# Attention with hashed masks and a gated MLP on one core: the product with v once per half of the queries

## The chip, the cores and the metric

One core of a Trainium2 chip runs the whole program. The metric is the device time of one execution in microseconds, as the median of several runs. The engines go by short names: PE (TensorE, matmuls), PEld (its weight loads), DVE (VectorE), ACT (ScalarE), POOL (GpSimd) and SP (SyncE, which issues most DMAs). SBUF is the working memory; PSUM, into which PE writes, has eight banks of 128 partitions x 512 numbers of 4 bytes.

## The reference

```python
# attention: q, k, v (4, 8, 768, 64), proj (64, 6)
q_bucket, k_bucket = number made of the 6 bits (x @ proj > 0)
mask   = q_bucket[:, :, :, None] == k_bucket[:, :, None, :]
scores = np.where(mask, q @ k.T / sqrt(64), -1e9)
scores = scores - max over the keys
attn   = exp(scores); attn = attn / (sum over the keys + 1e-9)
x      = attn @ v, heads side by side                  # (4, 768, 512)

# gated MLP
h    = gelu_tanh(x @ w_in)                             # 512 -> 1024
u, v = halves of h
v_n  = (v - mean) / sqrt(var + 1e-6) * g_ln
v_s  = einsum('ts,bsd->btd', w_sg, v_n) + b_sg         # mixes the 768 positions
out  = x + (u * v_s) @ w_out
```

Everything is 32-bit floats. The kernel splits most operands into a high part of reduced precision and a remainder, so that one exact product is two to four cheaper matmuls.

## The kernel before

**Order.** The kernel first collects all its work as groups (`plan.add(engine, cost, prio, fn, reads, writes)`) and then lets `Plan.order` write one order for every engine: a list scheduler with a planned duration for each group. At each step it takes the engine and the group that can start earliest, and among the groups that can start then (or a little later, `SOON`) the one with the lowest `prio`, its due time. The planned durations change no instruction, only this order; on the chip each engine then works through its own list in order and waits on semaphores where an operand or a buffer isn't ready. For PE the planner adds `TURN_PE` when a group's `form` differs from that of the group before. There are three forms before the change: `"row"` (64 rows of the array per matmul, two heads side by side), `"col"` (64 columns, two heads side by side) and `None` (everything else).

**Buffers.** `ring(shape, dtype, tag, bufs)` gives tiles that reuse one another in turn: the tile number i waits until all users of number i - bufs are through. `plan.slot` gives a PSUM bank out of a set instead; the planner picks the bank that is free first. Of several groups of an engine that want such a bank and could otherwise start, only the one with the lowest `prio` may be taken.

**Attention.** Two heads make a pair; 16 pairs, each with two halves of 384 queries, so 32 halves. `prepare` loads q and k, transposes and splits them (`parts`, L476 to L483) and computes the hash features (`features`, L498 and L501), which are extra rows that push a score down where the buckets differ. `largest` (L518, L525) computes scores with queries as rows, 384 keys at a time, and reduces the maximum on DVE; `shift` (L533 to L546) writes the maxima of a half back as a feature row. `weigh` (L562 to L583) then handles a chunk: two blocks of 128 keys by 384 queries and two heads. It computes the scores with keys as rows (four matmul pairs for each block), takes the exp on ACT into four tiles `p`, multiplies them with v into the accumulator `av` (L574, `product`), and adds them up over the keys on POOL (`sum`, L583). A half has three chunks, so `product` is called three times per half, each time for two of the six key blocks, all accumulating into `av`. `v` has a column for the mean and `p` a column of ones beside its 384. `finish` (L599 to L622) sums over partitions (`total`, L599), copies `av` out (`un`, L604), inverts the sums by way of small DMAs through DRAM (`s`, `sq`, `r`, `rs`) and writes the half of x to DRAM.

The due times: chunk number g is due at 2g, its product `AVP` = 3.75 later, `finish` `FINP` = 1.7 later, and the maxima run `AHEAD` = 5 chunks ahead. The 16 pieces of w_in (`weight_job`, L339 to L366, mostly on DVE) are spread over the pairs.

PSUM in this stage: one bank for `av` (pool `ps_t`, `NAV` = 1), seven banks that all other tiles share (pool `ps_s`, tags g0 to g6, `ps_tile`). The tiles `p` are a ring of 16.

**MLP.** For each of four batches: `load_x` (L687 to L692), `hidden_v` (L757 to L773: matmuls, gelu, layer norm), `hidden_u` (L789: matmuls and gelu), `gate` (L807 to L818) and `project` (L833 to L843). `hidden_v` of batch 0 comes at the end of the attention (`HID`) and still uses the seven shared banks. Then the attention's pools close, and the MLP has its own PSUM pools: `ps_h` as a ring of four banks, `ps_vs` as a ring of two (both in pool `pm`) and `ps_o` as a ring of two (pool `po`). With batch 0, w_sg is transposed and split (`gate_weights`, L708 to L725) and w_out is split (`out_weights`, `weight_job` again, tiles with names from `ow` on).

Of the kernel before, what the change touches and what calls it, by code (L numbers as in the profile page):

```python
# [25 lines left out]
NAV = 1  # L26
# [7 lines left out]
class Plan:  # L34
# [8 lines left out]
    TURN_PE = 0.09  # L43
# [59 lines left out]
    def order(self):  # L103
# [32 lines left out]
        while len(out) < len(G):  # L136
# [26 lines left out]
            if e == "PE":  # L163

                work = g["c"] + (self.TURN_PE if g["form"] != form else 0.0)
# [58 lines left out]
def kernel(  # L224
# [179 lines left out]
    ps_t, ps_s = Pool("ps_t", "left", PSUM), Pool("ps_s", "left", PSUM)  # L404
    ftp = ps_t.pool.tile([P, 512], F32, tag="av", name="ftp", bufs=NAV)
# [12 lines left out]
    if True:  # L418
        def w_tile(shape, dt, tag):
            return early.ring(shape, dt, tag)  # L420

        ps_slots = {i: 0.0 for i in range(8 - NAV)}

# [13 lines left out]
        NPT = 16  # L437
# [29 lines left out]
        def parts(st, s, prio):  # L467

            hh, lo, raw, fac = st.hi[s], st.lo[s], st.raw[s], (SCALE, 1.0)[s]
            for hf in range(2):  # L470
# [15 lines left out]
                plan.add(PE, 0.38, prio, tr, [raw, (hh, hf), (lo, hf)], [tp])  # L486
# [3 lines left out]
        def features(st, s, prio):  # L490
            hh, lo, ft = st.hi[s], st.lo[s], st.ft[s]
            for hf in range(2):
# [11 lines left out]
                plan.add(PE, 0.58, prio, project, [(hh, hf), (lo, hf), (ft, hf)], [fp])  # L504
                plan.add(DVE, 0.67, prio, sign, [fp], [(ft, hf)])

        def largest(st, t, prio):
# [13 lines left out]
            for kh in range(2):  # L521
                plan.add(PE, 0.36, prio + 0.01 * kh, lambda kh=kh: mm(kh),
                         [(st.hi[0], hf), (st.hi[1], kh), (st.ft[0], hf), (st.ft[1], kh)], sc[kh], form="row")
                for j in range(2):
                    plan.add(DVE, 0.56, prio, lambda j=j, kh=kh: nc.vector.tensor_reduce(  # L525
                        mx()[:, kh, i, j:j + 1], sc[kh][j]()[:, :SH], axis=AX.X, op=ALU.max, negate=True),
                        [sc[kh][j]], [(mx, (kh, j, i))])

        def shift(st, hf, prio):
# [12 lines left out]
            plan.add(PE, 0.35, prio, spread, [m], [tp])  # L542
# [5 lines left out]
        def weigh(st, hf, k0, prio):  # L548

            cs, two = slice(hf * SH, (hf + 1) * SH), (k0, k0 + 1)  # L550
            if k0 == 0:
                st.av = ps_t.ring([P, 512], F32, "av", NAV)
                st.sum = [late.ring([P, SH], F32, "sum", 4) for _ in range(2)]
            av, sums = st.av, st.sum
# [9 lines left out]
            for i, kt in enumerate(two):  # L564
                plan.add(PE, 0.71, prio + 0.01 * i, lambda i=i: mm(i),
                         [(x, hf) for x in (qh, ql, qf)] + [(x, kt // HT) for x in (kh, kl, kf)], sc[i], form="row")
                for j in range(2):
                    plan.add(ACT, 0.53, prio, lambda i=i, j=j: nc.scalar.activation(p[i][j]()[:, :SH], sc[i][j]()[:, :SH], AF.Exp),  # L568
                             [sc[i][j]], [p[i][j]])

            def product():
                for i, kt in enumerate(two):
                    for j in range(2):
                        nc.tensor.matmul(av()[row(j), :SH + 1], st.v()[:, j, kt, :], p[i][j](), start=(kt == 0), stop=(kt == NT - 1))  # L574

            plan.add(PE, 1.48, prio + AVP, product, p[0] + p[1] + [st.v], [av], form="col")
            for i, kt in enumerate(two):
# [3 lines left out]
                for j in range(2):  # L581
                    def add(j=j, i=i, e=e, first=p[0][j] if kt == 1 else sums[j]):
# [3 lines left out]
                             [sums[j]], port=True)  # L586

        def finish(st, hf, prio):
# [12 lines left out]
            plan.add(PE, 0.6, prio, total, sums, [tp])  # L601
# [50 lines left out]
        for n in range(NPAIR):  # L652
            for c in range(NT):
# [5 lines left out]
                if c % HT == HT - 1:  # L659
                    finish(sts[n], hf, 2 * g + FINP)  # L660
# [4 lines left out]
    b3 = pm = po_ = None  # L665
# [16 lines left out]
    def load_x(b, prio):  # L682
        r = []
        for c in range(NC):
# [7 lines left out]
            plan.add(ACT, 0.73, prio + c, lambda x=x, xh=xh: nc.scalar.copy(xh(), x()), [x], [xh])  # L692
            plan.add(M_["xl"], 1.76 if M_["xl"] == POOL else 0.87, prio + c, low, [x, xh], [xl])
# [9 lines left out]
    def gate_weights(prio):  # L703

        sg_v = w_sg.rearrange("(p t) s -> t p s", t=NT)
        for t in range(NT):
            w = tile_of([P, S], F32, "gs", 2 * NF)
            dma(prio + t - 5, 1.09, lambda eng, w=w, t=t: eng.dma_start(w(), sg_v[t]), w=[w], e=ACT)  # L708
            for hf in range(2):
# [17 lines left out]
                plan.add(PE, 0.32, prio + t, tr, [w], [tp])  # L727
# [9 lines left out]
    def gelu2(ps, dst, n, prio, key=None):  # L737

        h2 = tile_of([P, FH], F32, "h2", 2)
        us = n / 960.0  # L740
        plan.add(ACT, us - 0.02, prio, lambda: nc.scalar.activation(h2()[:, :n], ps()[:, :n], AF.Square), [ps], [h2])  # L741
        plan.add(DVE, us + 0.07, prio, lambda: nc.vector.scalar_tensor_tensor(  # L742
            h2()[:, :n], h2()[:, :n], 1.0 / GA, ps()[:, :n], op0=ALU.add, op1=ALU.mult), [h2, ps], [h2])
        plan.add(ACT, us - 0.02, prio, lambda: nc.scalar.activation(h2()[:, :n], h2()[:, :n], AF.Tanh, scale=GC * GA),
# [4 lines left out]
    def hidden_v(xx, prio):  # L749
        zh, zl = tile_of([P, NT, FH], F32R, "zh", 1), tile_of([P, NT, FH], F32R, "zl", 1)  # L750
        for t in range(NT):
            ps, p0 = ps_of("h", 4), prio + t
            ts_ = slice(t * P, (t + 1) * P)
            for c, (xh, xl) in enumerate(xx):
# [4 lines left out]
                plan.add(PE, 0.65, p0 + 0.01 * c, mm, [xh, xl], [ps])  # L759
# [4 lines left out]
            plan.add(DVE, 0.6, p0, lambda y=y, st=st: V.bn_stats(st(), y()), [y], [st])  # L764
# [140 lines left out]
```

## Time and profile before

| | |
|---|---|
| median of 3 runs | 830.72 us (828.22 to 831.31) |
| profiled execution: span from the first to the last instruction | 829.1 us; its own time isn't given beside the span |
| instructions | 15354 |
| busy PE / DVE / POOL / ACT | 795.1 / 602.3 / 449.5 / 415.3 us |
| granted clock of PE, mean | 0.988 of full speed |
| HBM read, written | 47.16 MB, 12.78 MB |
| last product with v (L574) starts | 486.1 us |

PE's busy time is a union of matmul spans, and matmuls are pipelined: a matmul is shown as longer than its share of the engine, and successive ones overlap. What one costs is read from the distance of the starts. A row such as "L574 PE MATMUL av<-p,v 128\*64 128x385" says: line 574, the tile written and those read, the part of the array used (rows\*columns), the shape of the result; one matmul call of 32-bit floats there is recorded as two instructions. The idle time at the end of a row is that of the engine just before the row's instructions, with what ended it.

### The profile page before, as it was taken

To read this page: it belongs to the slowest core of one execution; us is meant where nothing else is said; L and a number is where in the kernel's file an instruction comes from. 1 tells how busy PE (TensorE), PEld (TensorE's weight loads), DVE (VectorE), ACT (ScalarE), POOL (GpSimd) and SP (SyncE) were. 2 spreads that over 40 slices of the span, in tenths; PEclk is the share of its full clock that TensorE was granted. 3 is DMA by queue.
4 is the path that set the end of the run, shared out by engine and by line. 5 is a ranking of instruction groups with operands and counts; after the bars stand their busy time and mean duration, and the time that the engine had idled before them with its cause. 6 is when DMAs were issued, how large, how long until landed. Compare 5 with 4: busy or idle time off the path is not lost.

```text
span 829.1 us, 15354 instructions
## 1 busy us (share of the span) xinstructions
PE 795.1 (96%) x5480; PEld 613.1 (74%) x5480; DVE 602.3 (73%) x1241; ACT 415.3 (50%) x926; POOL 449.5 (54%) x470
## 2 busy tenths in 40 slices
PE   6999999999999999999999997799799999999998
PEld 4766666666666676667667666698689889988996
DVE  6998889998989888998768538888943248516730
ACT  2456566565566656656665655613343135314411
POOL 1478887889868877787887862333105201601130
PEclk9899999999999999999999999799999999999999
DMA  5222441441442233133222011610024220131003
GB/s 152 51 51 74 107 122 34 111 127 36 113 110 57 73 97 91 34 110 78 60 58 60 21 40 41 223 45 25 27 83 134 82 90 1 39 106 47 1 1 127
DMA packets 99308, 60.94 MB, mean 74 GB/s; under 512 B 64288, under 2 KB 91040, under 8 KB 99232
## 3 DMA queue, kind: packets, MB, share of 16 engines
q1 hardware_dynamic: 97920, 56.94, 24.6%
q10 hardware_dynamic: 1312, 3.02, 1.0%
q8 instruction: 43, 0.70, 0.4%
q14 instruction: 33, 0.27, 0.2%
HBM read 47.16 MB, written 12.78 MB: 72 GB/s over the span
## 4 chain that ended last, share of the span: by engine, by line
PE 75%; DVE 19%; DMA 3%; issue 1%; ACT 1%; SPq 1%; DVEq 0%; ACTq 0%
PE g L562 15%; PE av L574 13%; PE ps_vs L807 12%; PE ps_o L833 8%; PE g L518 7%; PE ps_h L789 6%; DVE mx L525 5%; PE ps_h L757 4%; PE g L498 4%; PE g L476 2%; PE g L757 2%; PE g L540 1%; PE g L599 1%; PE ps_o L838 1%; DVE m L534 1%
## 5 line engine op out<-in xcount | busy, mean ns | idle before, releaser
L583 POOL TENSOR_TENSOR sum<-sum,p 128x384 f32<-128x384 f32 x256 | 260.7, 1049 | 61.1 <-ACT p L568 61.0
L525 DVE TENSOR_REDUCE mx<-g 128x1 f32<-128x384 f32 x384 | 187.7, 547 | 51.8 <-PE g L518 51.6
L568 ACT ACTIVATE p<-g 128x384 f32<-128x384 f32 x384 | 160.5, 494 | 104.9 <-PE g L562 97.4
L574 PE MATMUL av<-p,v 128*64 128x385 f32 x768 | 145.4, 500 | 0.0
L574 PEld LDWEIGHTS av<-p,v 128*64 128x64 f32 x768 | 46.6, 136 | 57.2 <-issue 53.6
L562 PE MATMUL g<-hq,hk 64*128 64x384 f32 x384 | 79.8, 389 | 2.4 <-DVE mx L525 2.4
L562 PEld LDWEIGHTS g<-hq,hk 64*128 64x128 f32 x384 | 39.5, 185 | 51.2 <-issue 26.7
L518 PE MATMUL g<-fk,fq 64*128 64x384 f32 x384 | 76.2, 360 | 0.5 <-DVE fk L501 0.2
L742 DVE SCALAR_TENSOR_TENSOR h<-h,ps_h 128x384 f32<-128x384 f32 (+1 forms) x50 | 29.1, 596 | 65.1 <-ACT h L741 64.8
L767 POOL TENSOR_TENSOR mv<-mv,epsr 128x1 f32<-128x1 f32 x24 | 14.8, 619 | 107.6 <-DVE mv L766 107.6
L518 PE MATMUL g<-hk,hq 64*128 64x384 f32 x384 | 71.6, 340 | 0.0
L583 POOL TENSOR_TENSOR sum<-p,p 128x384 f32<-128x384 f32 x64 | 64.3, 1026 | 10.4 <-ACT p L568 10.4
L562 PE MATMUL g<-hq,lk 64*128 64x384 f32 x384 | 68.9, 336 | 0.0
L562 PE MATMUL g<-lq,hk 64*128 64x384 f32 x384 | 68.7, 335 | 0.0
L562 PE MATMUL g<-fq,fk 64*128 64x384 f32 x384 | 68.6, 335 | 0.0
L833 PE MATMUL ps_o<-woh,gs 128*128 128x512 f32 x192 | 65.5, 402 | 0.0
L807 PE MATMUL ps_vs<-wgh,zl 128*128 128x384 f32 x192 | 64.3, 335 | 0.3 <-DVE zl L773 0.3
L807 PE MATMUL ps_vs<-wgh,zh 128*128 128x384 f32 x192 | 64.3, 335 | 0.0
L807 PE MATMUL ps_vs<-wgl,zh 128*128 128x384 f32 x192 | 64.2, 334 | 0.0
L818 POOL TENSOR_TENSOR gs<-gt,gs 128x384 fp32r<-128x384 f32 x32 | 33.3, 1043 | 55.0 <-ACT gs L815 55.0
L690 POOL TENSOR_TENSOR xl<-x,xh 128x768 fp32r<-128x768 f32 x16 | 30.1, 1890 | 47.6 <-ACT xh L692 38.3
L789 PE MATMUL ps_h<-xh,wih 128*128 128x384 f32 x128 | 44.7, 349 | 9.7 <-DVE y L746 8.2
(135 smaller groups left out, 1729.7 us busy)
## 6 DMA issues: line engine op xcount, KB each, us to landing
q<-in_q_dram SPq DMA_DIRECT2D x32, 192.0 KB
k<-in_k_dram SPq DMA_DIRECT2D x32, 192.0 KB
v<-in_v_dram SPq DMA_DIRECT2D x16, 384.0 KB
rs<-r SPq DMA_DIRECT2D x64, 96.0 KB
xs<-xt SPq DMA_DIRECT2D x32, 192.0 KB
x<-xs SPq DMA_DIRECT2D x16, 384.0 KB
rx<-xs SPq DMA_DIRECT2D x96, 64.0 KB
out_dram<-ob SPq DMA_DIRECT2D x24, 256.0 KB
```

What stands on the lines that cost most here:

```text
L498: nc.tensor.matmul(fp()[:, :SH], w[:, s, :], x()[:, cs], start=(i == 0), stop=(i == 2))
L518: nc.tensor.matmul(sc[kh][j]()[:, :SH], x[0]()[row(j), qs], x[1]()[row(j), kh * SH:(kh + 1) * SH], start=(n == 0), stop=(n == 1))
L525: plan.add(DVE, 0.56, prio, lambda j=j, kh=kh: nc.vector.tensor_reduce(mx()[:, kh, i, j:j + 1], sc[kh][j]()[:, :SH], axis=AX.X, op=ALU.max ...
L562: nc.tensor.matmul(sc[i][j]()[:, :SH], x()[row(j), ks], y()[row(j), cs], start=(n == 0), stop=(n == 3))
L568: plan.add(ACT, 0.53, prio, lambda i=i, j=j: nc.scalar.activation(p[i][j]()[:, :SH], sc[i][j]()[:, :SH], AF.Exp), [sc[i][j]], [p[i][j]])
L574: nc.tensor.matmul(av()[row(j), :SH + 1], st.v()[:, j, kt, :], p[i][j](), start=(kt == 0), stop=(kt == NT - 1))
L583: (nc.gpsimd if e == POOL else nc.vector).tensor_add(sums[j](), first()[:, :SH], p[i][j]()[:, :SH])
L757: nc.tensor.matmul(ps(), x()[:, ts_], w[:, c, FH:FF], start=(c == 0 and n == 0), stop=(c == NC - 1 and n == 2))
L789: nc.tensor.matmul(ps()[:, :SH], w[:, c, fs], x()[:, cs], start=(c == 0 and n == 0), stop=(c == NC - 1 and n == 2))
L807: nc.tensor.matmul(vp(), z()[:, t, fs], w()[:, t, cs], start=(t == 0 and n == 0), stop=(t == NT - 1 and n == 2))
L818: nc.gpsimd if e == POOL else nc.vector).tensor_sub(gl()[:, cs], gt(), gh()[:, cs].bitcast(F32)),
L833: nc.tensor.matmul(po(), a()[:, ts_], w()[:, f, :], start=(f == 0 and n == 0), stop=False)
```

## The change

1. The product with v leaves `weigh`. A new function `weighted` is called once per half, behind its third chunk, and multiplies all six key blocks in one group of 12 calls. The 12 `p` tiles of a half are held until then; their ring grows from 16 to 17. The due time is the same 3.75 behind the third chunk.
2. The accumulator `av` is no longer a bank of its own: it is taken from the shared set like any other tile. The set has eight banks, and the MLP uses the same set throughout: the pools `ps_t`, `pm` and `po` and the rings of four, two and two are gone.
3. Planned durations: new figures for most groups, among them a turn cost that depends on the form that is entered, and a form of its own for `total`.

```diff
-NAV = 1
-    TURN_PE = 0.09
+    TURN_PE = {"row": 0.2, "col": 0.14, "col32": 0.14, None: 0.14}
-                work = g["c"] + (self.TURN_PE if g["form"] != form else 0.0)
+                work = g["c"] + (self.TURN_PE[g["form"]] if g["form"] != form else 0.0)
...
-    ps_t, ps_s = Pool("ps_t", "left", PSUM), Pool("ps_s", "left", PSUM)
-    ftp = ps_t.pool.tile([P, 512], F32, tag="av", name="ftp", bufs=NAV)
+    ps_s = Pool("ps_s", "left", PSUM)
+    ftp = ps_s.pool.tile([P, 512], F32, tag="g0", name="ftp", bufs=1)
...
-        ps_slots = {i: 0.0 for i in range(8 - NAV)}
+        ps_slots = {i: 0.0 for i in range(8)}
...
-        NPT = 16
+        NPT = 17
...
             if k0 == 0:
-                st.av = ps_t.ring([P, 512], F32, "av", NAV)
-                st.sum = [late.ring([P, SH], F32, "sum", 4) for _ in range(2)]
-            av, sums = st.av, st.sum
+                st.sum, st.p = [late.ring([P, SH], F32, "sum", 4) for _ in range(2)], []
+            sums = st.sum
...
-            def product():
-                for i, kt in enumerate(two):
-                    for j in range(2):
-                        nc.tensor.matmul(av()[row(j), :SH + 1], st.v()[:, j, kt, :], p[i][j](), start=(kt == 0), stop=(kt == NT - 1))
-
-            plan.add(PE, 1.48, prio + AVP, product, p[0] + p[1] + [st.v], [av], form="col")
+            st.p += p
...
+        def weighted(st, prio):
+
+            st.av, p = ps_tile(), st.p
+            av = st.av
+
+            def product():
+                for kt in range(NT):
+                    for j in range(2):
+                        nc.tensor.matmul(av()[row(j), :SH + 1], st.v()[:, j, kt, :], p[kt][j](), start=(kt == 0), stop=(kt == NT - 1))
+
+            plan.add(PE, 1.3 * HT, prio, product, [t for two in p for t in two] + [st.v], [av], form="col")
...
-            plan.add(PE, 0.6, prio, total, sums, [tp])
+            plan.add(PE, 0.375, prio, total, sums, [tp], form="col32")
...
                 if c % HT == HT - 1:
+                    weighted(sts[n], 2 * g + AVP)
                     finish(sts[n], hf, 2 * g + FINP)
...
-    b3 = pm = po_ = None
+    b3 = None
...
     def ps_of(tag, bufs, shape=(P, FH)):
-        if pm is None:
-            return ps_tile()
-        return (po_ if tag == "o" else pm).ring(list(shape), F32, "ps_" + tag, bufs)
+        return ps_tile()
...
-    end = ps_s.close()
-    pm = Pool("pm", "right", PSUM, end)
-    end = ps_t.close(end)
-    po_ = Pool("po", "right", PSUM, end)
```

Planned durations (us), before and after:

| group | before | after |
|---|---|---|
| transposes of q, k / features, PE | 0.38 / 0.58 | 0.327 / 0.522 |
| scores for the maxima / for the exps, PE | 0.36 / 0.71 | 0.346 / 0.692 |
| maximum, DVE / exp, ACT | 0.56 / 0.53 | 0.55 / 0.495 |
| product, PE | 1.48 three times | 3.9 once |
| spread / total, PE | 0.35 / 0.6 | 0.33 / 0.375 |
| x split: ACT / POOL | 0.73 / 1.76 | 0.83 / 1.88 |
| hidden_v / hidden_u / gate / project, PE | 0.65 / 0.49 / 0.49 / 0.65 | 0.696 / 0.522 / 0.52 / 0.685 |
| w_sg transposes, PE | 0.32 | 0.36 |
| gelu of n columns: ACT, DVE | n/960 - 0.02, n/960 + 0.07 | n/1100 + 0.135 (square) or + 0.155 (tanh), n/960 + 0.15 |
| layer norm: statistics, scale, high part, low part | 0.6, 0.66, 0.6, 0.66 | 0.69, 0.75, 0.72, 0.76 |
| gate: bias, times u (DVE), high (ACT), low (POOL) | 0.47, 0.47, 0.4, 0.96 | 0.56, 0.56, 0.51, 1.03 |
| output copy, ACT | 0.5 | 0.59 |

Due times, `AHEAD`, the engines that each piece runs on and the arithmetic are the same.

More of the change, by code (lines that the diff above doesn't have):

```diff
@@ L521, in largest @@
             for kh in range(2):
-                plan.add(PE, 0.36, prio + 0.01 * kh, lambda kh=kh: mm(kh),
+                plan.add(PE, 0.346, prio + 0.01 * kh, lambda kh=kh: mm(kh),
                          [(st.hi[0], hf), (st.hi[1], kh), (st.ft[0], hf), (st.ft[1], kh)], sc[kh], form="row")
                 for j in range(2):
-                    plan.add(DVE, 0.56, prio, lambda j=j, kh=kh: nc.vector.tensor_reduce(
+                    plan.add(DVE, 0.55, prio, lambda j=j, kh=kh: nc.vector.tensor_reduce(
                         mx()[:, kh, i, j:j + 1], sc[kh][j]()[:, :SH], axis=AX.X, op=ALU.max, negate=True),
@@ L540, in spread @@
                     nc.tensor.matmul(tp()[:, i * P:(i + 1) * P], m()[:, i, :], identr, start=True, stop=True)
-            plan.add(PE, 0.35, prio, spread, [m], [tp])
+            plan.add(PE, 0.33, prio, spread, [m], [tp])
             ft, cs = st.ft[0], slice(hf * SH, (hf + 1) * SH)
@@ L690, in low @@
                 (nc.gpsimd if M_["xl"] == POOL else nc.vector).tensor_sub(xl(), x(), xh().bitcast(F32))
-            plan.add(ACT, 0.73, prio + c, lambda x=x, xh=xh: nc.scalar.copy(xh(), x()), [x], [xh])
-            plan.add(M_["xl"], 1.76 if M_["xl"] == POOL else 0.87, prio + c, low, [x, xh], [xl])
+            plan.add(ACT, 0.83, prio + c, lambda x=x, xh=xh: nc.scalar.copy(xh(), x()), [x], [xh])
+            plan.add(M_["xl"], 1.88 if M_["xl"] == POOL else 0.87, prio + c, low, [x, xh], [xl])
             r.append((xh, xl))
@@ L758, in mm @@
                                          stop=(c == NC - 1 and n == 2))
-                plan.add(PE, 0.65, p0 + 0.01 * c, mm, [xh, xl], [ps])
+                plan.add(PE, 0.696, p0 + 0.01 * c, mm, [xh, xl], [ps])
             y = tile_of([P, FH], F32, "y", 2)
@@ L763, in hidden_v @@
             V = nc.vector
-            plan.add(DVE, 0.6, p0, lambda y=y, st=st: V.bn_stats(st(), y()), [y], [st])
+            plan.add(DVE, 0.69, p0, lambda y=y, st=st: V.bn_stats(st(), y()), [y], [st])
             plan.add(DVE, 0.08, p0, lambda st=st, mv=mv: V.bn_aggr(mv()[:, 0:2], st()), [st], [mv])
@@ L768, in hidden_v @@
                                                                            op=ALU.pow), [mv], [mv])
-            plan.add(DVE, 0.66, p0, lambda y=y, mv=mv: V.scalar_tensor_tensor(
+            plan.add(DVE, 0.75, p0, lambda y=y, mv=mv: V.scalar_tensor_tensor(
                 y(), y(), mv()[:, 0:1], g_bc(), op0=ALU.subtract, op1=ALU.mult), [y, mv, g_bc], [y], port=True)
-            plan.add(ACT, 0.6, p0, lambda y=y, mv=mv, t=t: nc.scalar.mul(zh()[:, t, :], y(), mv()[:, 2:3]),
+            plan.add(ACT, 0.72, p0, lambda y=y, mv=mv, t=t: nc.scalar.mul(zh()[:, t, :], y(), mv()[:, 2:3]),
                      [y, mv], [(zh, t)])
-            plan.add(DVE, 0.66, p0, lambda y=y, mv=mv, t=t: V.scalar_tensor_tensor(
+            plan.add(DVE, 0.76, p0, lambda y=y, mv=mv, t=t: V.scalar_tensor_tensor(
                 zl()[:, t, :], y(), mv()[:, 2:3], zh()[:, t, :].bitcast(F32), op0=ALU.mult, op1=ALU.subtract),
@@ L806, in mm @@
                         for n, (z, w) in enumerate(((zh, wgh), (zh, wgl), (zl, wgh))):
-                            nc.tensor.matmul(vp(), z()[:, t, fs], w()[:, t, cs], start=(t == 0 and n == 0),
+                            nc.tensor.matmul(vp()[:, :SH], z()[:, t, fs], w()[:, t, cs], start=(t == 0 and n == 0),
                                              stop=(t == NT - 1 and n == 2))
-                    plan.add(PE, 0.49, p0 + 0.01 * t, mm, [(zh, t), (zl, t), wgh, wgl], [vp])
-                plan.add(DVE, 0.47, p0, lambda vp=vp, gt=gt, cs=cs: nc.vector.tensor_add(gt(), vp(), b_bc()[:, cs]),
+                    plan.add(PE, 0.52, p0 + 0.01 * t, mm, [(zh, t), (zl, t), wgh, wgl], [vp])
+                plan.add(DVE, 0.56, p0, lambda vp=vp, gt=gt, cs=cs: nc.vector.tensor_add(gt(), vp()[:, :SH], b_bc()[:, cs]),
                          [vp, b_bc], [gt])
                 e = M_["gm"]
-                plan.add(e, 0.96 if e == POOL else 0.47, p0, lambda gt=gt, f=f, cs=cs, e=e: (
+                plan.add(e, 1.03 if e == POOL else 0.56, p0, lambda gt=gt, f=f, cs=cs, e=e: (
                     nc.gpsimd if e == POOL else nc.vector).tensor_mul(gt(), gt(), us[f]()[:, cs]), [gt, (us[f], hf)], [gt], port=True)
-                plan.add(ACT, 0.4, p0, lambda gt=gt, gh=gh, cs=cs: nc.scalar.copy(gh()[:, cs], gt()), [gt], [(gh, hf)])
+                plan.add(ACT, 0.51, p0, lambda gt=gt, gh=gh, cs=cs: nc.scalar.copy(gh()[:, cs], gt()), [gt], [(gh, hf)])
                 e = M_["gl"]
-                plan.add(e, 0.96 if e == POOL else 0.47, p0, lambda gt=gt, gh=gh, gl=gl, cs=cs, e=e: (
+                plan.add(e, 1.03 if e == POOL else 0.56, p0, lambda gt=gt, gh=gh, gl=gl, cs=cs, e=e: (
                     nc.gpsimd if e == POOL else nc.vector).tensor_sub(gl()[:, cs], gt(), gh()[:, cs].bitcast(F32)),
@@ L841, in project @@
             plan.add(PE, 0.43, p0 + 0.1, residual, [rx], [po])
-            plan.add(ACT, 0.5, p0, lambda ob=ob, po=po: nc.scalar.copy(ob(), po()), [po], [ob])
+            plan.add(ACT, 0.59, p0, lambda ob=ob, po=po: nc.scalar.copy(ob(), po()), [po], [ob])
             dma(p0, 0.73, lambda eng, ob=ob, t=t: eng.dma_start(ov[:, t, :], ob()), [ob])
@@ L872 @@
     plan.run(tc)
-    for p in (b3, b2, b1, po_, pm):
+    for p in (b3, b2, b1, ps_s):
         p.pool.release()
```

20 lines of the change are left out of this document (10 added, 10 removed).

## The prediction

> **What bounds the kernel now.** I read the page first: the busy shares, the slices and the chain that ended last.
>
> ```profile
> PE 795.1 (96%) x5480; PEld 613.1 (74%) x5480; DVE 602.3 (73%) x1241; ACT 415.3 (50%) x926; POOL 449.5 (54%) x470
> ...
> PE   6999999999999999999999997799799999999998
> ...
> DVE  6998889998989888998768538888943248516730
> ...
> PE 75%; DVE 19%; DMA 3%; issue 1%; ACT 1%; SPq 1%; DVEq 0%; ACTq 0%
> PE g L562 15%; PE av L574 13%; PE ps_vs L807 12%; PE ps_o L833 8%; PE g L518 7%; PE ps_h L789 6%; DVE mx L525 5%; PE ps_h L757 4%; PE g L498 4%; PE g L476 2%; PE g L757 2%; PE g L540 1%; PE g L599 1%; PE ps_o L838 1%; DVE m L534 1%
> ```
>
> TensorE is busy nearly everywhere and holds 75% of the chain. VectorE holds 19% and is close to full through the attention, which is the first 24 slices. So I cut the span at the stage borders; the columns are busy microseconds (instructions) of PE, weight loads, DVE, ACT and POOL, then the granted clock and the DMA.
>
> ```profile
> 100.00:200.00 100.00, 97.02 (x804) 65.77 (x800) 90.25 (x173) 64.16 (x153) 81.36 (x81) 1.00 0.32 88
> 200.00:300.00 100.00, 98.73 (x812) 67.69 (x813) 89.58 (x171) 61.08 (x148) 76.87 (x79) 1.00 0.35 90
> 300.00:400.00 100.00, 97.96 (x812) 66.12 (x812) 86.82 (x166) 60.88 (x147) 78.16 (x79) 1.00 0.29 75
> 400.00:486.00 86.00, 85.96 (x715) 56.45 (x709) 54.24 (x107) 55.14 (x132) 71.66 (x73) 1.00 0.18 48
> 505.00:605.00 100.00, 85.19 (x429) 77.39 (x429) 87.93 (x216) 42.01 (x87) 29.58 (x39) 0.93 0.23 76
> 605.00:830.00 225.00, 220.43 (x1161) 199.98 (x1159) 96.34 (x183) 73.96 (x135) 47.59 (x45) 1.00 0.21 65
> ```
>
> In the attention (to about 486) TensorE is the bound, with VectorE some ten per cent behind it. From 505 to 605 TensorE is idle for 14.8 us and VectorE is the fuller one. After 605 TensorE is alone again. A saving on TensorE inside the attention therefore counts, until VectorE is full.
>
> **Term 1: fewer products.** First the cost of one product, from the timeline of TensorE and of its weight loads (start, duration, in us):
>
> ```profile
> 212.27 0.34 PE L518 MATMUL g<-fk,fq 64*128 64x384 f32 x2
> 212.44 0.34 PE L518 MATMUL g<-hk,hq 64*128 64x384 f32 x2
> 212.72 1.51 PE L574 MATMUL av<-p,v 128*64 128x385 f32 x8
> 213.09 0.14 PEld L574 LDWEIGHTS av<-p,v 128*64 128x64 f32 x2 [0.18 <-issue]
> 213.41 0.14 PEld L574 LDWEIGHTS av<-p,v 128*64 128x64 f32 x2 [0.18 <-issue]
> 214.16 0.44 PE L562 MATMUL g<-hq,hk 64*128 64x384 f32 x2
> 214.44 0.34 PE L562 MATMUL g<-hq,lk 64*128 64x384 f32 x2
> 214.61 0.35 PE L562 MATMUL g<-lq,hk 64*128 64x384 f32 x2
> ```
>
> Score matmuls (64*128, two side by side in the rows of the array) start 0.17 apart: 212.27, 212.44, and 214.44, 214.61. The four calls of a product appear as 8 matmuls in four pairs, and the weight loads of successive pairs start 0.32 apart; the plan's new figure for four pairs is 1.3, and I take it. From 212.44 to 214.44 are 2.00 us: one score step, the product, one score step. Overhead of the change of form there and back: 2.00 - 2 x 0.17 - 1.30 = 0.36 us. The matmuls themselves stay: 768 before and after.
>
> ```profile
> L574 PE MATMUL av<-p,v 128*64 128x385 f32 x768 | 145.4, 500 | 0.0
> ...
> 204.47 0.82 PE L476 MATMUL g<-ident,k 128*128 128x128 f32 x6
> 205.22 1.51 PE L574 MATMUL av<-p,v 128*64 128x385 f32 x8
> 206.66 0.53 PE L599 MATMUL g<-sum,ones 128*32 128x192 f32 x8
> ```
>
> 768 / 8 = 96 products, three for each of 32 halves. After the change there are 32 with 24 matmuls each, so 64 visits to the other form go. Not each removes two changes between scores and product: the one at 205.22 stands between transposes and the sums, which differ from one another anyway, and there only its own tail, 1.44 - 1.30 = 0.14, is sure to go. Ends: 64 x 0.14 = 9.0 and 64 x 0.36 = 23.0. Most lie between scores as in the first fence, so I take 0.30: **-19.2 us**, all of it in TensorE's own order of work, with nothing else lying beside it.
>
> **Term 2: VectorE in the attention.** What TensorE waits for there now, and what VectorE does in 55 to 400 (columns of the second fence as in the stage table; of the third: count, busy, mean ns, idle before):
>
> ```profile
> PE g L540 <- DVE m L534: 3.5, 6, 1.1
> PE g L562 <- DVE mx L525: 2.4, 5, 0.7
> PE g L476 <- DVE mx L525: 1.5, 1, 1.5
> ```
>
> ```profile
> 55.00:400.00 345.00, 337.62 (x2785) 229.91 (x2785) 303.95 (x581) 212.53 (x509) 270.63 (x272) 1.00 0.33 86
> ```
>
> ```profile
> L525 DVE TENSOR_REDUCE mx<-g 128x1 f32<-128x384 f32 x280 | 137.1, 547 | 33.8 <-PE g L518 33.6
> L620 DVE TENSOR_TENSOR xt<-un,rs 128x384 f32<-128x384 f32 x23 | 16.9, 734 | 0.8 <-DMA rs<-r 0.8
> ```
>
> The waits are 7.4 us. In the stretch of 345 us are 23 halves (one L620 each). Each loses 2 x 0.30 = 0.60, so it shrinks by 13.8 to 331.2, VectorE goes from 88% to 92%, and its idle time from 41.0 to 27.2. If waits grow as that idle time shrinks (41.0 / 27.2 = 1.5), they become 11.1: **+4 us**. Ends: -7.4 (no wait is left; the eighth bank is free for scores except while a product and its copy hold it) and +13.8 (VectorE's idle time can't shrink at all). POOL, 270.63 of 345, would go to 82%. Its additions are no later relative to anyone: what waits for them is the total, once per half, and a tile is reused only 17 exps later.
>
> The product now needs a bank that it must win like any other tile; before it had its own. It holds one for 12 pairs, 3.9 us, and the copy L604 frees it, so seven banks remain for scores meanwhile, as many as now, and eight otherwise. I cost that at nothing, covered by the same seven banks.
>
> The exps: 12 of 17 tiles of a half are held until its product, five are left, and the next chunk takes four. The product's due time (3.75 behind its last chunk's, chunks 2 apart) puts it behind one further chunk and ahead of the second one, so exps need not wait: 0. The one more tile and its memset: 0, at the start beside the DMA wait.
>
> **Term 3: shared banks behind the attention.** TensorE's waits from 486 to 620, and the stretches at half clock:
>
> ```profile
> PE ps_h L789 <- DVE y L746: 8.2, 5, 3.9
> PE ps_h L716 <- DVE wgl L725: 2.8, 3, 2.3
> PE ps_h L716 <- DVE u L746: 1.9, 2, 1.0
> PE ps_h L789 <- DVE u L746: 1.6, 1, 1.6
> ```
>
> ```profile
> 530.00:540.28 10.28, 7.72 (x31) 6.17 (x30) 9.72 (x19) 6.08 (x14) 6.18 (x5) 0.50 0.42 130
> 598.30:601.70 3.40, 3.29 (x10) 3.29 (x11) 3.30 (x10) 1.06 (x4) 0.95 (x2) 0.50 0.01 2
> ```
>
> ```profile
> 506.71 0.44 PE L789 MATMUL ps_h<-xh,wih 128*128 128x384 f32 x1 [1.01 <-DVE y L746]
> ...
> 510.90 0.45 PE L789 MATMUL ps_h<-xh,wih 128*128 128x384 f32 x1 [1.83 <-DVE y L746]
> ...
> 517.00 0.44 PE L789 MATMUL ps_h<-xh,wih 128*128 128x384 f32 x1 [1.58 <-DVE u L746]
> ```
>
> Each of these is a matmul that waits for the reader of a bank in a ring of four (ps_h), while the banks of ps_vs and ps_o stand empty. With one set of eight, TensorE can run four tiles further ahead; the three waits shown, 1.0 + 1.8 + 1.6 = 4.4, come first in the stage and go. The later ones sit behind VectorE, 87.93 of 100 us busy with work that the change does not touch: when banks come free, what is late next is VectorE's gelu and weight splitting. After waits the clock falls to half: of 7.72 and 3.29 busy us at 0.50, half (5.5) is lost. Ends: 0, and -12 (VectorE's idle time in that stretch). I take **-5**.
>
> **Term 4: planned durations.** They change no instruction, only the order that the planner writes. Several come closer to the rows: exp goes from 0.53 to 0.495, and the page has 494 ns.
>
> ```profile
> L568 ACT ACTIVATE p<-g 128x384 f32<-128x384 f32 x384 | 160.5, 494 | 104.9 <-PE g L562 97.4
> ```
>
> No row shows the new order. A better one can only take waits that terms 2 and 3 hold already; a worse one costs at worst, by the nearest rows, another place like the longest now, 3.9 of waiting with 1.6 of lost clock behind it: 0 to +5.5, I take 0.
>
> **Sum.** 829.1 - 19.2 + 4 - 5 + 0 = 808.9 against the profiled span. The median of the runs, 830.72, is 1.6 above that span (they go from 828.22 to 831.31), so about **810 us** for the median. Half a per cent, 4.2 us, is what I count as no change: 826.6 to 834.9.
>
> **Rivals.** *VectorE takes the saving.* Up to 400 its idle time stays at 41 us because a larger share is forced by the long product; then only the thinner end gains.
>
> ```profile
> 400.00:490.00 90.00, 31.81 (x168) 10.19 (x168) 1.00 0.18 48
> ```
>
> 168 / 8 = 21 products there (this view counts L574 alone), 14 removed, 4.2 us; with term 3, 829.1 - 4.2 - 5 + 1.6 = 821.5. For it: 90% busy at 100 to 300. Against it: it waited 33.6 us on scores alone. The Trainium skill, TensorEngine Tiling (Array Packing), section Performance Considerations, warns that tiling speeds up TensorE and not the emptying of PSUM, which may become the bottleneck; the 88% agrees that this is near, not that it is reached. By that rule alone the time is the 821.5 of this rival.
>
> *Slower: the long product starves VectorE.* From the last score for a maximum to the next stand a product of 3.9 + 0.36 and a weigh of eight steps, 1.4: 5.7 us, in which VectorE has at most four tiles of 0.547, 2.2 us. The other 3.5 must come from its remaining work, (303.95 - 137.1) / 23 = 7.3 us per half, part of which needs banks too. Its idle time per half is 41.0 / 23 = 1.8 now. The point that decides: if more than 1.8 stay idle per half, the attention is longer than before. With 2.6 unfilled, 0.8 x 32 = 26: 829.1 + 26 - 5 + 1.6 = 852.
>
> *Exps wait for tiles.* If the plan puts the product behind the second chunk, its exps wait for the ring of 17 and hold banks. With 0.6 us per half the saving is spent: 829. Nothing in the profile speaks for it but the five tiles.
>
> *More.* Term 3 gives its whole 12 and term 2 nothing: 829.1 - 19.2 - 12 + 1.6 = 799.5.
>
> **Chances.** The forecast 0.54 (803 to 818 by itself), VectorE takes it 0.18, more 0.13, exps 0.07, slower 0.08. The range 797 to 826 leaves out the last two and the edges of the others, 0.2. Faster: 0.54 + 0.13 + 0.15 of the second = 0.82; same: 0.03 + 0.06 = 0.09; slower 0.08 + 0.01 = 0.09.
>
> **What would show it.** The timeline should show L574 as x24 in one piece, the next form's first start 12 x 0.325 + 0.14, about 4.0 us, behind the product's. Term 2: PE's waits for L525 and L534 near 11 us and DVE 92% busy; 20 us or more would mean the first rival, long idle time of L525 behind every product the second, L568 waiting for L574 the third. Term 3: no wait of L789 in the first tiles behind the attention. Wrong would make it above all a VectorE that can't run at 92% under bursts, or a new order behind the attention that waits elsewhere.

## The result and the profile after

The changed kernel takes 811.1 us (median of 4 runs, 810.48 to 813.27), against 830.32 (4 runs) for the kernel before: a ratio of 0.977 with a 95% interval of 0.975 to 0.979. The profiled execution has a span of 808.6 us and took 810.48 itself; before, the span was 829.1. So 20.5 us went between the two spans. The forecast was 810.

The page of the changed kernel, with the slices of PE and DVE and the chain:

```profile
PE 777.6 (96%) x5480; PEld 627.0 (78%) x5480; DVE 594.6 (74%) x1241; ACT 410.9 (51%) x926; POOL 446.9 (55%) x471
...
PE   6999999999899999999999999699899999999998
...
DVE  7889988797988988988998449878981268407730
...
PE 79%; DVE 17%; DMA 1%; issue 1%; ACT 1%; ACTq 0%; SPq 0%; DVEq 0%
```

The work is the same number of matmuls in less time, and TensorE's share of the chain that ended last has risen from 75% to 79%. The stages, in the columns of the stage table of the prediction:

```profile
100.00:200.00 100.00, 97.73 (x834) 70.54 (x832) 84.82 (x164) 63.26 (x152) 84.53 (x84) 1.00 0.35 91
200.00:300.00 100.00, 94.06 (x791) 70.75 (x789) 88.35 (x169) 59.38 (x143) 77.29 (x78) 0.95 0.32 85
300.00:400.00 100.00, 99.06 (x853) 71.48 (x855) 88.92 (x179) 64.35 (x157) 82.63 (x84) 1.00 0.31 78
476.00:586.00 110.00, 100.59 (x511) 91.84 (x508) 92.01 (x223) 51.07 (x101) 33.90 (x43) 0.92 0.23 71
586.00:809.00 223.00, 218.97 (x1153) 198.61 (x1151) 101.36 (x201) 74.54 (x139) 46.82 (x48) 1.00 0.21 67
```

The count of matmuls in 100 us (behind PE's busy time) shows the gain: 834 and 853 where there were 804 and 812. The stretch 200 to 300 is worse than before, 791 for 812, with the clock at 0.95. A product in the timeline of TensorE of the changed kernel:

```profile
450.47 0.34 PE L517 MATMUL g<-hk,hq 64*128 64x384 f32 x2
450.74 4.10 PE L589 MATMUL g<-p,v 128*64 128x385 f32 x24
454.77 0.55 PE L539 MATMUL g<-identr,m 128*128 128x128 f32 x3
455.25 0.44 PE L560 MATMUL g<-hq,hk 64*128 64x384 f32 x2
```

It is one block of 24, and the next form starts 4.03 us behind it; three products of before took 3 x 1.44 = 4.32 by the same measure, and had six changes of form in place of two. What TensorE waits for now:

```profile
PE g L560 <- DVE mx L524: 8.1, 8, 3.3
PE g L475 <- DMA q<-in_q_dram: 4.7, 2, 4.1
PE g L720 <- DVE wgl L729: 4.0, 2, 3.3
PE g L793 <- DVE y L750: 3.0, 1, 3.0
...
PE g L720 <- DVE u L750: 1.1, 1, 1.1
PE g L517 <- DVE mx L524: 0.8, 2, 0.6
PE g L517 <- ACT p L566: 0.8, 2, 0.5
...
PE g L475 <- DVE mx L524: 0.3, 1, 0.3
```

To see where the 20.5 us went I divided the distance from each matmul's start to the next one's over the whole trace into three parts: the idle time that the view of waits names, half of what else lies at half clock, and the rest, which is work together with changes of form and with waits too short to show as idle. The last column is explained below.

| us | before | after | merged product alone | seven banks | x later |
|---|---|---|---|---|---|
| work, changes of form, short waits | 786.1 | 761.6 | 778.4 | 774.4 | 758.5 |
| of it at the borders between forms | 35.9 | 16.4 | 15.6 | 13.2 | 14.7 |
| of it short waits between score matmuls | 11.8 | 10.2 | 22.9 | 24.8 | 5.9 |
| named waits | 27.8 | 24.4 | 39.0 | 30.5 | 22.6 |
| lost to half clock | 9.0 | 16.4 | 16.3 | 11.8 | 12.3 |
| span (with the ends, 6.3) | 829.1 | 808.6 | 840.0 | 823.0 | 799.6 |

("At the borders" is what a step out of a score, feature or product matmul into another form takes above its ordinary step, with a product taken as a whole; "short waits" is what a step between two score matmuls takes above 0.17 us for a pair.) Between before and after, work falls by 24.5, waits by 3.4, and half clock takes back 7.4.

The two rows "of it" depend on what counts as an ordinary step. By a wider count, in which the first score step behind a change and the first step of a product belong to the border too, the borders are 39.7 before, 16.7 after and 16.8 with the merged product alone, a fall of 23.0 in place of 19.5; the short waits are then 12.2, 13.0 and 26.9, and 28.8 with seven banks.

By place, from each trace (it is cut at the first and at the last matmul with v; the ends, 6.3, are left out):

| us | before | after | merged product alone | merged, new durations, old banks | seven banks | rings in the MLP | x later |
|---|---|---|---|---|---|---|---|
| up to the first | 32.9 | 36.8 | 38.0 | 36.6 | 35.4 | 37.1 | 36.7 |
| from the first to the last (attention) | 450.8 | 436.8 | 456.0 | 449.5 | 446.6 | 436.7 | 419.8 |
| behind the last | 339.0 | 328.7 | 339.7 | 341.9 | 334.8 | 336.2 | 336.8 |

The columns behind "before" are described where their runs come. Of the 10.3 us that the stretch behind the last product lost, some 3 are 15 matmuls of `hidden_v` that now stand ahead of it (an estimate from their planned 0.7 us for three).

### The profile page after: what moved, and what is told of

Same layout as the page of the kernel before. It is cut to its first block, busy times and chain, and to the rows that moved or that the text cites. A ratio compares the mean times of both kernels' runs of the same rounds, so it can differ in the third digit from the quotient of the medians.

```text
span 808.6 us, 15333 instructions
## 1 busy us (share of the span) xinstructions
PE 777.6 (96%) x5480; PEld 627.0 (78%) x5480; DVE 594.6 (74%) x1241; ACT 410.9 (51%) x926; POOL 446.9 (55%) x471
## 4 chain that ended last, share of the span: by engine, by line
PE 79%; DVE 17%; DMA 1%; issue 1%; ACT 1%; ACTq 0%; SPq 0%; DVEq 0%
PE g L560 16%; PE g L589 13%; PE g L811 12%; PE g L837 8%; PE g L517 7%; PE g L761 6%; PE g L793 5%; PE g L497 4%; DVE mx L524 3%; PE g L475 3%; PE g L604 2%; PE g L539 1%; PE g L842 1%; DVE h L746 1%; DVE wx L363 1%
## 5 line engine op out<-in xcount | busy, mean ns | idle before, releaser
L576 POOL TENSOR_TENSOR sum<-sum,p 128x384 f32<-128x384 f32 x256 | 257.4, 1041 | 41.0 <-ACT p L566 40.8
L566 ACT ACTIVATE p<-g 128x384 f32<-128x384 f32 x384 | 161.4, 495 | 53.5 <-PE g L560 49.5
L589 PE MATMUL g<-p,v 128*64 128x385 f32 x768 | 131.2, 491 | 0.0
L589 PEld LDWEIGHTS g<-p,v 128*64 128x64 f32 x768 | 52.3, 137 | 64.5 <-issue 61.4
L822 POOL TENSOR_TENSOR gs<-gt,gs 128x384 fp32r<-128x384 f32 x32 | 32.9, 1031 | 76.2 <-ACT gs L819 76.2
L576 POOL TENSOR_TENSOR sum<-p,p 128x384 f32<-128x384 f32 x64 | 67.0, 1065 | 14.3 <-ACT p L566 14.3
L560 PE MATMUL g<-hq,lk 64*128 64x384 f32 x384 | 74.6, 343 | 0.0
L746 DVE SCALAR_TENSOR_TENSOR h<-h,g 128x384 f32<-128x384 f32 (+1 forms) x56 | 32.6, 605 | 55.0 <-ACT h L745 55.0
L837 PE MATMUL g<-woh,gs 128*128 128x512 f32 x192 | 65.4, 401 | 0.0
L811 PE MATMUL g<-wgh,zl 128*128 128x384 f32 x192 | 64.3, 335 | 0.0
L811 PE MATMUL g<-wgh,zh 128*128 128x384 f32 x192 | 64.3, 335 | 0.0
L811 PE MATMUL g<-wgl,zh 128*128 128x384 f32 x192 | 64.2, 334 | 0.0
L814 DVE TENSOR_TENSOR gt<-g,b_bc 128x384 f32<-128x384 f32 x32 | 17.8, 555 | 52.8 <-PE g L811 32.4
L609 ACT COPY un<-g 128x385 f32<-128x385 f32 x32 | 15.4, 480 | 79.2 <-PE g L589 75.6
```

What stands on the lines that cost most here:

```text
L560: nc.tensor.matmul(sc[i][j]()[:, :SH], x()[row(j), ks], y()[row(j), cs], start=(n == 0), stop=(n == 3))
L566: plan.add(ACT, 0.495, prio, lambda i=i, j=j: nc.scalar.activation(p[i][j]()[:, :SH], sc[i][j]()[:, :SH], AF.Exp), [sc[i][j]], [p[i][j]])
L576: (nc.gpsimd if e == POOL else nc.vector).tensor_add(sums[j](), first()[:, :SH], p[i][j]()[:, :SH])
L811: nc.tensor.matmul(vp()[:, :SH], z()[:, t, fs], w()[:, t, cs], start=(t == 0 and n == 0), stop=(t == NT - 1 and n == 2))
L822: nc.gpsimd if e == POOL else nc.vector).tensor_sub(gl()[:, cs], gt(), gh()[:, cs].bitcast(F32)),
L837: nc.tensor.matmul(po(), a()[:, ts_], w()[:, f, :], start=(f == 0 and n == 0), stop=False)
```

## The experiments

**One part alone.** The change has three parts, so I ran each alone, and then each pair. First the merged product:

```diff
-            plan.add(PE, 1.48, prio + AVP, product, p[0] + p[1] + [st.v], [av], form="col")
+            st.p += p
...
+            st.av, p = ps_t.ring([P, 512], F32, "av", NAV), st.p
...
+            plan.add(PE, 1.3 * HT, prio, product, [t for two in p for t in two] + [st.v], [av], form="col")
```

> The kernel before with the merged product alone: one product per half, 17 tiles, but the accumulator's own bank, the MLP's own rings and the old planned durations (the group's own cost is 3.9). Theory (the visits to the other form cost TensorE 0.3 to 0.36 us each, 64 go): 806 to 814 us, and the sum of the distances between matmul starts, without waits and at full clock, falls by 19 to 23 us. Rival (the gain is one of order and banks, and without them VectorE takes the saving): 822 us or more, with TensorE's waits for VectorE in the attention up by over 12 us.

It measured 841.4 us, a ratio of 1.014 (1.011 to 1.017): slower, and beyond the rival's 822, though the waits in the attention rose by 8.7 (7.3 to 16.0) and not by its 12. The borders between forms did fall, by 20.3 us (35.9 to 15.6). But short waits between scores rose by 11, so that work as a whole fell by 7.7 and not by the 19 to 23 expected, named waits rose by 11 and half clock by 7. The waits of TensorE's weight loads, first in the kernel before and then with the merged product alone (total, times, longest):

```profile
PEld g L562 <- DVE mx L525: 7.5, 14, 0.9
...
PEld g L518 <- DVE mx L525: 6.3, 21, 0.6
```

```profile
PEld g L562 <- DVE mx L525: 17.0, 28, 2.5
...
PEld g L518 <- DVE mx L525: 7.0, 19, 2.7
```

The scores wait for the maxima's reader twice as often. The starving of the prediction's second rival has a part in it: VectorE is idle for 21.4 of the 131.2 us of products, before for 11.8 of 145.4. But with old banks and new durations (below) it is 14.3 and with seven shared banks 9.8, and their attention is long too. What the three have in common is the mirror image: between two products TensorE fills banks faster than they come free, and scores wait for them. By the wider count these short waits are 26.9, 26.0 and 28.8 us, against 12.2 before and 13.0 in the changed kernel.

The banks alone, with three products per half:

> The kernel before with the eight shared banks alone: three products per half in one shared bank, the MLP from the same set, old planned durations. Theory (the banks are worth only the waits of L789 and of the transposes of w_sg behind the attention): 822 to 828 us, matmul work unchanged within 3 us, those waits down from 14.8 to 9 or less. Rival (the banks carry half of the gain): 820 us or less.

829.8 us, ratio 1.000 (0.999 to 1.002), a miss: the waits of L789 fell from 9.8 to 3.8 us, as expected, but under the old durations the plan put other waits behind them (gate and hidden layer of the next batch), and in all the kernel waited no less, 29.6 us after 27.8. The durations alone:

> The kernel before with the new planned durations alone (1.3 for each of three products per half). Theory (no instruction changes, only order): 826 to 834 us, no change beyond half a per cent. Rival (a better order is what made the kernel faster): 822 us or less.

828.1 us, ratio 0.998 (0.997 to 0.999): no change by the bound of half a per cent. And the other direction, the product six times per half:

```diff
-            def product():
-                for i, kt in enumerate(two):
+            for i, kt in enumerate(two):
+                def product(i=i, kt=kt):
...
-            plan.add(PE, 1.48, prio + AVP, product, p[0] + p[1] + [st.v], [av], form="col")
+                plan.add(PE, 0.83, prio + AVP - 1 + 1 * i, product, p[i] + [st.v], [av], form="col")
```

> The kernel before with the product once per key block, six times per half (192 visits to the other form instead of 96), everything else as before. Theory (each visit costs 0.14 to 0.36 us of TensorE's own time): 96 x 0.14 to 0.36 = 13 to 35 more, 844 to 865 us, unless two visits stand next to one another in the order, which would cost nothing. Rival (a visit's cost hides in the pipeline and only the order matters): within 4 us of before.

842.5 us, ratio 1.015 (1.013 to 1.016). It is close to the theory's low end of 844, and not for its reason: the plan put most of the 192 products next to one another, only 22 more visits were left, and work stayed at 785.4. The time went into a wait that had little to do with the form, here in TensorE's waits of this run (before, 3.5 in the attention):

```profile
PE g L540 <- DVE m L534: 10.5, 11, 1.4
```

So this run says nothing on the price of a visit.

**Two parts together.** The three parts alone come to +11.5, +0.2 and -1.5 us by their ratios, +10.2 in all, where the change measured -19.2. They must act on one another, so I ran the pairs:

> The changed kernel with the old planned durations (merged product and shared banks, the product group at 3.9). The merged product alone came out 1.4% slower, although its changes of form fell as planned: waits, short hidden waits between score matmuls and half clock took more than was saved. Theory B (what it lacked were banks to feed VectorE through a product of 4 us): 808 to 816 us. Rival D (what it lacked was an order written with durations that fit): 830 us or more.

> The changed kernel with the old banks (merged product and new durations, a bank of its own for the accumulator, seven for the rest, the MLP's own rings). Theory B (banks were lacking): 828 us or more, with TensorE's waits and short waits in the attention as in the merged product alone. Rival D (the order was): 810 to 818 us, the turns saved and only the waits behind the attention back.

> The changed kernel with three products per half (shared banks and new durations). Both theories: no turn is saved, so 822 to 831 us; it would be far below that only if banks and durations together, without the merging, made the gain.

| merged | shared banks | durations | us | ratio to before (95%) |
|---|---|---|---|---|
| - | - | - | 829.5 | 1 |
| yes | - | - | 841.4 | 1.014 (1.011 to 1.017) |
| - | yes | - | 829.8 | 1.000 (0.999 to 1.002) |
| - | - | yes | 828.1 | 0.998 (0.997 to 0.999) |
| yes | yes | - | 815.5 | 0.984 (0.981 to 0.987) |
| yes | - | yes | 836.3 | 1.009 (1.006 to 1.012) |
| - | yes | yes | 818.7 | 0.989 (0.986 to 0.992) |
| yes | yes | yes | 811.1 | 0.977 (0.975 to 0.979) |

(Each ratio is against runs of the kernel before that were taken beside it, with medians from 829.45 to 830.32.)

Theory B holds and D falls: merging needs the banks (-3.0 points with old durations, -3.2 with new ones), and neither set of durations replaces them. The last row but one was not foreseen by either: banks and durations without merging are worth 1.1 points, about half of the gain's 2.3. Given both, merging adds 1.2 points, some 10 us.

**Which banks?** The shared set does two things: the attention has eight in place of seven and one, and the MLP has eight in place of four, two and two. First one bank less:

```diff
-        ps_slots = {i: 0.0 for i in range(8)}
+        ps_slots = {i: 0.0 for i in range(7)}
```

> The changed kernel with seven shared banks in place of eight, the eighth unused throughout. Theory B (between two products the scores need the eighth bank): 826 us or more; waits of TensorE in the attention and short hidden waits between score matmuls together 15 us or more above the changed kernel's. Rival S (what counts is not the number but that the product takes its bank from the set, and that the MLP shares): 816 us or less.

824.1 us, ratio 0.994 (0.991 to 0.996), so 1.7 points of the gain need the eighth bank: by the table by place 9.8 us of it in the attention and 6.1 behind it, where the MLP lacks the bank too. The total lies just under theory B's bound of 826 and far from the rival's 816. Short waits between scores rise by 14.6 and named waits in the attention by 3.1, 17.7 together, where 15 or more was expected.

Which moment counts shows against the run with the old banks and new durations. There the scores have seven banks at all times; here they have seven between products and six during one, since the product holds one of the seven. Yet the attention takes 446.6 us here and 449.5 there. With eight shared banks, eight between products and seven during one, it takes 436.8. So the banks between the products decide, and one bank less during a product cost nothing that these runs show. (The planner knows how many banks there are, so the order differs between these runs too.)

The timeline of TensorE shows the waits, here between two products of this run:

```profile
322.75 0.35 PE L517 MATMUL g<-hk,hq 64*128 64x384 f32 x2
322.94 0.61 PE L560 MATMUL g<-hq,hk 64*128 64x384 f32 x2
323.12 0.43 PE L560 MATMUL g<-hq,lk 64*128 64x384 f32 x1
323.39 0.33 PE L560 MATMUL g<-lq,hk 64*128 64x384 f32 x1
323.40 0.34 PE L560 MATMUL g<-hq,lk 64*128 64x384 f32 x1
...
326.22 0.69 PE L560 MATMUL g<-hq,hk 64*128 64x384 f32 x2 [2.13 <-DVE mx L524]
```

The two matmuls of a pair, one for each head, usually stand in one row as x2 and start together. At 323.12 the pairs come apart: the second head's weight load waited for an exp (ACT, L566), and its matmul of that step follows 0.28 later. No idle time is named there, because the other head's matmul covers it. Then, at 326.22, both wait 2.1 us.

The Trainium skill, Perfetto Trace Analysis, section Matmul Optimizations, asks to use all eight PSUM banks. The runs agree: with one of eight left unused, the changed kernel loses 1.7 points. They add a condition: the kernel before uses all eight as well, one of them for `av` alone, and to share that one brought nothing (1.000) until the products were merged.

Then the MLP's rings put back, with the attention as changed:

> The changed kernel with the MLP's own rings of four, two and two banks behind the attention, which keeps its eight shared ones. Theory (the MLP's part of the banks is worth the waits of L789 there): 815 to 820 us, 4 to 9 more, all of it behind the last product. Rival (the MLP's banks are worth nothing, all the gain of the banks is in the attention): 813 us or less.

818.0 us, ratio 0.987 (0.985 to 0.988): 1.0 point, within the expectation. The last matmul with v starts at 476.1 here and at 476.0 in the changed kernel, so all of it is behind the attention: 336.2 us against 328.7, with the same matmuls. TensorE's waits for banks of the ring in this run:

```profile
PE ps_h L795 <- DVE u L752: 8.8, 2, 5.1
...
PE ps_h L795 <- DVE y L752: 2.6, 2, 2.0
```

**The place of the product.** The prediction costed the ring of 17 tiles at nothing as long as the product stands ahead of the second further chunk. Here it is due later:

```diff
-AVP = 3.75
+AVP = 4.5
```

> The changed kernel with the product due 4.5 behind its last chunk in place of 3.75, behind the scores of the second further chunk. Theory (its exps need the tiles that the product still holds, the third rival of the prediction): 825 us or more, with long waits of ACT's exps for the product. Rival (the first matmuls of the product free the first tiles soon, and five tiles reach): 815 us or less.

836.7 us, ratio 1.008 (1.006 to 1.011). The theory holds; the wait shows elsewhere than I wrote. In the trace the scores of two further chunks, eight tiles, are computed ahead of 31 of the 32 products, and when such a product ends, five of their exps have run and never a sixth: 12 + 5 is the ring of 17. The other three scores keep their banks. Their exps stand behind the copy of the accumulator in ACT's order, so ACT's wait is booked on that copy. The first row is from the waits of the changed kernel, the second from those of this run:

```profile
ACT un L609 <- PE g L589: 75.6, 27, 4.0
```

```profile
ACT un L609 <- PE g L589: 126.4, 31, 5.3
```

Ahead of that copy ACT idles 126 us in 31 halves, 4.1 each, as long as a product; in the changed kernel it is 2.8 each.

**The longest wait.** The bad stretch of the changed kernel is 200 to 300. Its timeline on DVE and POOL with the first scores behind it, and then the two longest stretches at half clock:

```profile
210.54 0.98 DVE L361 TENSOR_SCALAR wy<-wx 128x256 int32<-128x256 int32 x1
211.33 1.85 POOL L694 TENSOR_TENSOR xl<-x,xh 128x768 fp32r<-128x768 f32 x1
211.56 1.91 DVE L362 SCALAR_TENSOR_TENSOR wy<-w,wy 128x256 f32<-128x256 uint32 x1
213.50 0.42 DVE L363 TENSOR_TENSOR wx<-wx,wy 128x256 f32<-128x256 f32 x1
213.84 1.02 DVE L524 TENSOR_REDUCE mx<-g 128x1 f32<-128x384 f32 x2
...
214.44 0.68 PE L560 MATMUL g<-hq,hk 64*128 64x384 f32 x1 [3.31 <-DVE mx L524]
```

```profile
213.56:223.81 10.25, 9.37 (x55) 8.04 (x57) 9.61 (x17) 6.46 (x15) 5.02 (x5) 0.50 0.16 50
510.50:524.20 13.70, 9.71 (x37) 8.22 (x38) 13.46 (x31) 10.06 (x24) 5.83 (x6) 0.50 0.45 161
```

That step of splitting w_in, from the view of its line in the changed kernel and then in the next run (duration in ns: least, median, longest; then first and last start):

```profile
L362 DVE SCALAR_TENSOR_TENSOR wy<-w,wy x16: 414/426/1906, 15.0 to 433.1; 128x256 f32<-128x256 uint32 x16
```

```profile
L362 DVE SCALAR_TENSOR_TENSOR wy<-w,wy x16: 424/426/427, 14.9 to 417.4; 128x256 f32<-128x256 uint32 x16
```

At 211.56 it takes 1.91 us where the median is 0.43, and ends with POOL's subtraction of x (L694, 1.85 us). The maxima wait behind it on DVE, the scores for the maxima, and the clock then stays at half for 10.25 us, in which 9.37 us of TensorE's time do half the work: wait and clock are 3.3 + 4.7 = 8 us. Of the 3.3 the stretched step made 1.5 at most; the rest is the other steps ahead of the maximum. The Trainium skill, SBUF — State Buffer, section Who interferes with whom, says that a VectorE instruction with two inputs in SBUF contends with a GpSimd instruction that reads SBUF, for a shared port pair that is locked; the end of L362 behind that of L694 agrees. L694 isn't alone: of the 32 instructions of L361 and L362 on w_in, ten are stretched in the changed kernel, two behind L694 alone, one beside L694 and an addition, and seven beside POOL's additions (L576, L626), at 0.7 to 1.1 us.

To test that, the plan was told that batch 0's loads of x also need what pair 12 writes. That adds no instruction; POOL's four subtractions move from 114 to 211 us to 433 to 450 us.

```diff
-            dma(prio + c, 1.09, lambda eng, x=x, c=c: eng.dma_start(x(), xs[b][c]), [xd[b][c]], [x])
+            dma(prio + c, 1.09, lambda eng, x=x, c=c: eng.dma_start(x(), xs[b][c]), [xd[b][c]] + ([xd[3][0]] if b == 0 else []), [x])
```

> The changed kernel, with the loads of x for batch 0 listed in the plan as reading the row block that pair 12 writes, so that they and their splitting (ACT and POOL) come after pair 12 and not from pair 4 on; no instruction is added. Theory (the longest wait of TensorE in the changed kernel, 3.3 us at 211 with 10 us at half clock behind it, comes from POOL's subtraction of x falling among VectorE's splitting of w_in): no such wait around 211, 801 to 808 us. Rival (VectorE's splitting runs into POOL's additions there as well, and another place takes its turn): 808 to 813 us, with waits of the scores for the maxima still at 8 us or more and a half-clock stretch elsewhere in the attention.

801.2 us, ratio 0.965 (0.963 to 0.966). In the waits and the windows of this run:

```profile
PE g L560 <- DVE mx L524: 4.0, 13, 0.4
```

```profile
39.00:460.00 421.00, 417.04 (x3625) 307.66 (x3623) 368.68 (x725) 268.15 (x658) 350.00 (x352) 1.00 0.31 81
200.00:224.00 24.00, 23.71 (x202) 16.80 (x200) 22.03 (x43) 14.98 (x38) 20.81 (x22) 1.00 0.35 87
```

The longest wait for a maximum is 0.4 us, the clock is full through the whole attention, and VectorE is busy 368.68 of 421, 88%. The last matmul with v starts at 458.9 in place of 476.0. Behind it the kernel is 8 us longer than the changed one, so 17 us of gain are worth about 9. (One step of splitting w_out now meets L694 there, at 581.8, and takes 1.81 us in place of 0.29.) The wait at 211 and the half clock behind it, 8 us, are gone; but so are all ten stretched steps, also those beside the additions: L361 and L362 took 19.5 us on w_in and take 11.5. So the move changed the order of the whole attention, and what L694 alone cost isn't shown. With seven banks no step of L361 and L362 on w_in is stretched either, and that kernel is slower all the same.

With the finishing due a little later, a wider choice in the planner and the next batch's x due earlier:

```diff
-MLP = {"xl": "POOL", "gm": "DVE", "gl": "POOL", "wg": 398.29, "wo": 46.93, "x": 568.79}
+MLP = {"xl": "POOL", "gm": "DVE", "gl": "POOL", "wg": 398.29, "wo": 46.93, "x": 548.1}
...
-PREP, SHIFTP, FINP, WSTEP, WP = 0.96, 0.15, 1.7, 12, 7.76
+PREP, SHIFTP, FINP, WSTEP, WP = 0.96, 0.15, 2.37, 12, 7.76
...
-    SOON = 0.11
+    SOON = 0.14
```

> As the run before, with the finishing due 2.37 behind its chunk in place of 1.7, a wider choice of groups that start soon (0.14 in place of 0.11), and x of the next batch due 20 earlier. Meant as the better version: 800 to 808 us if the order still holds waits that a plan can take out; 808 to 813 if they are VectorE's own.

800.1 us, ratio 0.963 (0.961 to 0.965), against the run before within the uncertainty of both. It is the fastest version here, 3.7% below the kernel before and 1.4 points below the change. A later finishing on the changed kernel itself (due 3.5 behind its chunk, forecast at 803 to 810 us) gave no measurement, so what the finishing's place is worth there stays open.

## Why the prediction was right, and where not

The median was forecast to about one microsecond, but that is partly luck: two terms were off in opposite directions, and one step failed. By place the forecast was -15 up to the last product and -5 behind it; measured were -10.1 and -10.3, of which some 3 us only moved from behind it to ahead of it.

**Term 1 was right.** Forecast -19.2 us (9.0 to 23.0) for 64 visits; the borders between forms fell by 19.5 (23.0 by the wider count). That merging alone lowers them by 20.3 confirms the price with the old banks and durations.

**The step that failed: the banks in the attention, costed at nothing, "covered by the same seven banks".** I compared the banks during a product, which are seven in both kernels, and not those between products. Merging takes away the pauses in which banks drained, so the seven of before are too few. With seven in the set the kernel is 1.7 points slower than with eight, and with the accumulator's own bank slower than the kernel before. In the attention, 9.8 of the 14.0 us saved hang on the eighth bank. The seven-bank kernel's 824.1 lies near the 821.5 of the first rival, but for another reason: that rival put VectorE at its limit, and what failed were banks. What TensorEngine Tiling (Array Packing) of the Trainium skill warns of in its section Performance Considerations, that emptying PSUM may become the bottleneck, shows in part with seven banks: the scores wait 24.8 us in short waits for their readers, 10.2 with eight.

**Term 2 was mis-sized.** Waits in the attention were to grow from 7.4 to 11.1; the rows give 8.1 + 0.8 + 0.8 + 0.3 = 10.0. But I put no clock beside them, and one wait of 3.3 us was followed by another 4.7 lost at half clock. With the start of the program, where the half-clock stretch grew from 6.8 to 10.2 us, the time up to the last product lost 6.5 us more to the clock than before. VectorE was to be busy for 92% of 55 to 400; in the changed kernel it is 303.84 of 345, 88% as before:

```profile
55.00:400.00 345.00, 335.45 (x2860) 246.26 (x2858) 303.84 (x591) 215.59 (x520) 279.45 (x280) 0.99 0.33 86
```

So its idle time there did stay at 41 us, as the first rival said, but the long product doesn't force it: with x later it is busy 318.12 of these 345 us, the forecast's 92%, with no instruction added or taken away, and the attention takes 420 us in place of 437.

**Term 3 was too small.** Forecast -5; the rings put back cost 7.5 us behind the last product, with the same matmuls there. Named waits behind the attention fell from 14.8 to 9.4, and the half clock there rose by 1.0: the transposes of w_sg still wait for VectorE (4.0 us), as the term said of the later ones.

**Term 4** was 0. Alone the durations give 0.998; with shared banks and three products they bring 1.1 points, and on top of merging and banks 0.7. As a term of a sum it was wrong, since its worth depends on what the other parts allow.

**The exps**: right at 3.75, where the rival had five tiles to speak for it; 0.75 later it came true, 26 us slower than the change.

## What to carry to other kernels

Fewer changes of form on TensorE are worth what their borders cost, 0.3 us for a way there and back here, but merging a product also removes the pauses in which VectorE and ScalarE empty PSUM (the attention took 446.6 us with seven shared banks, 436.8 with eight): count the banks between the long blocks, not only during them. Parts of a change that do nothing alone can be what makes another part work, so run them in pairs before dropping one. A wait of three microseconds on TensorE should be priced with the half clock behind it, here 3.3 us and then 4.7.

## What the runs showed of the hardware that I had not expected

Two heads' score matmuls that usually start together come apart when one bank is late, and the view of waits names no idle time for it: 24.8 us of such short waits with seven banks, against 10.2 with eight. And one VectorE instruction of 0.43 us that met a GpSimd one of 1.85 us took 1.91; the wait of 3.3 us behind it, and the half clock after that, came to 8 us. GpSimd's additions of about 1 us stretched the same instruction to about 1.1.
